# First token chunk of a gated projection split by hidden width: half of it between retention pairs, the rest after chunk two; weight conversion without Pool

## The chip, the cores and the metric

One core of one Trainium2 chip runs the whole program. The metric is device time in microseconds of one execution, median over several runs.

## What is computed

The reference is a retention layer followed by two feed-forward layers, in float32 (weights arrive as float64 words and are converted on the chip). Cut to what matters:

```python
# q, k, v: (4 batches, 8 heads, 576 positions, 64)
scores = q @ k.T / sqrt(64)
ret = scores * Dmat                 # Dmat[h,i,j] = gamma_h ** (i-j) for i >= j, else 0
x = (ret @ v) -> (2304 tokens, 512)
# feed-forward 1, d_ff = 1536
g = x @ w_gate;  val = x @ w_val
x = (g * sigmoid(g) * val) @ w_out  # (2304, 512)
# feed-forward 2, d_ff = 2048
r = maximum(x @ w_in, 0)
out = (r * r) @ w_out2              # (2304, 512)
```

## The kernel before, in words

**Retention.** Sixteen pairs (4 batches x 4 pairs of heads) run as a loop of 17 iterations; iteration n starts pair n and finishes pair n - 1. `load(n + 2)` issues the loads of q, k and v (`qk_sb`, `kv_sb`, four buffers each, L207 and L211) on SyncE's queue. `prep_state` scales k and q on Pool (L220, L224). `scores` multiplies k by q (L241) into a score tile `s` (two buffers of two PSUM banks), and VectorE multiplies it by the mask (L246). `state` accumulates k-v states (L265), ScalarE copies them to `sbd` (L270). `apply` multiplies q by the states and the masked scores by v (L283, L296), and ScalarE copies the result to `xy`, the activations, which stay on the chip, transposed (L301).

**Weight conversion.** A unit is a 128 x 512 tile of weights. There are 36 for phase one (for each of 12 slices f of the hidden width: gate g, value v, output o, in this order) and 32 for phase two (i and o for each of 16 slices). A unit is loaded as raw 64-bit words (L105; two buffers `raw_p`, and two more pieces lent from columns of `xy` while a chunk's activations there are no longer needed), then converted by the generator `conversion` in five steps: two ScalarE operations (L136, L137), then on VectorE a clamp (L139), a shift (L143), a merge of the sign bits (L145) and an addition of the low words, as two halves on VectorE (L151) for the first eight units and the odd ones, and as one operation on Pool (L153) for the other even ones. Then `parts_unit` splits the float into a rounded high part on ScalarE (L120) and the rest as a low part on Pool (L121). `pump(k)` advances the generator by k steps up to a limit; `ensure` runs it until a named unit exists.

**Projections.** Every product is done as three matmuls (high x high, high x low, low x high; `three`, L364 to L366). Tokens are in five chunks (four of 512 and one of 256). In phase one, a step (n, f) projects chunk n by the units g and v of slice f (24 matmuls of 512 columns), applies sigmoid on ScalarE (L405) and two products on VectorE (L407, L409), splits the hidden tile into high (L397, ScalarE) and low (L398, VectorE), and one step later `out1` multiplies it by unit o into four accumulators (12 matmuls); at the last f they are copied back to `xy`. The activations of the next chunk are split by `split_x` (L358, L359) behind the last projection of a chunk. Phase two works the same way with one projection a step, Relu and a square (L417, L419), and `out2`.

**Order.** The program order is the loop order below; the framework assigns each engine's queue at compile time from that order and a model of the times, so neighbours can change places. Eight units are converted during retention, one step at each of four places per iteration from iteration 3; the other 28 of phase one while chunk 0 is projected, four steps after each part of a step. The 32 units of phase two take the tiles that phase one's weights leave (`allowed`): 20 of them during the last chunk of phase one.

Weights live in two pools, `wa_p` (17 units, there from the start) and `wb_p` (19, in the space that retention's tiles leave).

Of the kernel before, what the change touches and what calls it, by code (L numbers as in the profile page):

```python
# [9 lines left out]
F32 = mybir.dt.float32  # L10
# [25 lines left out]
WA = 17  # L36
EARLY = 8
FROM = 3
PUMPS = {0: 1, 1: 4, 2: 1}
# [9 lines left out]
def retention_moe_kernel(  # L49
# [33 lines left out]
    order = [(1, what, f) for f in range(F1) for what in "gvo"]  # L83
# [24 lines left out]
    ring = {"n": 0}  # L108

    def weight_tiles():  # L110
        wp = wa_p if ring["n"] % (3 * F1) < WA else wb_p
        ring["n"] += 1
        hi = wp.tile([P, 512], F32R, tag="hi", name="w_hi")
        lo = wp.tile([P, 512], F32R, tag="lo", name="w_lo")
        return hi, lo

    def parts_unit(i):
        wf = w_t.pop(i).bitcast(F32)
        hi, lo = weight_tiles()
        nc.scalar.copy(hi, wf)  # L120
        nc.gpsimd.tensor_tensor(out=lo, in0=wf, in1=f32(hi), op=ALU.subtract)  # L121
        units[order[i]] = (hi, lo)

    def conversion():
        ts = nc.vector.tensor_scalar
        for i in range(len(order)):
# [22 lines left out]
            if i < EARLY or i % 2:  # L149
                for a in range(2):  # L150
                    nc.vector.tensor_tensor(out=w[:, a], in0=w[:, a], in1=low[:, a], op=ALU.add)  # L151
            else:
                nc.gpsimd.tensor_tensor(out=w, in0=w, in1=low, op=ALU.add)  # L153
# [23 lines left out]

    with ExitStack() as st:
# [133 lines left out]
        pumped["limit"] = 5 * EARLY  # L312
        for n in range(last + 2):
            new, old, nxt = n <= last, n > 0, n + 1 <= last
            fill = PUMPS[0] if n >= FROM else 0
            if n == FROM - 1:
                prefetch(1)
# [10 lines left out]
            if old:  # L328
                apply(n - 1, False)
# [8 lines left out]
            if old:  # L338
                apply(n - 1, True)


    wb_p = pool(ctx, "wb_p", 3 * F1 - WA)
    ps_g = pool(ctx, "ps_g", 2, space=PSUM)
    ps_a = pool(ctx, "ps_a", 1, space=PSUM)

    xs, xs_w = {}, []

    def split_x(ph, n, cc):
        t0, m = CHUNKS[ph][n]
        src = xy[:, cc, t0:t0 + m]  # L350
        if ph == 2 and n == 0:
            xs_w.append(weight_tiles())
        if ph == 2 and n % 2 == 0:
            hi, lo = cut(xs_w[cc], 0, m)
        else:
            hi = xs_p.tile([P, N], F32R, tag="xh", name="xh")[:, :m]
            lo = xs_p.tile([P, N], F32R, tag="xl", name="xl")[:, :m]
        nc.scalar.copy(hi, src)  # L358
        nc.vector.tensor_tensor(out=lo, in0=src, in1=f32(hi), op=ALU.subtract)  # L359
        xs[ph, n, cc] = (hi, lo)  # L360

    def three(dst, a, b, first, last):
        (ah, al), (bh, bl) = a, b
        nc.tensor.matmul(dst, ah, bh, start=first, stop=False)  # L364
        nc.tensor.matmul(dst, ah, bl, start=False, stop=False)  # L365
        nc.tensor.matmul(dst, al, bh, start=False, stop=last)  # L366

    def cut(pair, a, n):
        return tuple(x[:, a:a + n] for x in pair)

    def project(ph, n, f, *cols):
        for what, _ in cols:
            ensure((ph, what, f))
        parts = [
            (ps_g.tile([P, 512], F32, tag=tag, name=tag), units[ph, what, f]) for what, tag in cols
        ]
        last = f == (F1, F2)[ph - 1] - 1
        todo = [(ps, w, cc) for ps, w in parts for cc in range(CC)]
        split_after = ph == 1 and last and n + 1 < NCH
        if split_after:  # L380
            todo.sort(key=lambda x: x[2])
        for ps, w, cc in todo:
            three(ps[:, :CHUNKS[ph][n][1]], cut(w, cc * P, P), xs[ph, n, cc], cc == 0, cc == CC - 1)
        if split_after:
            for cc in range(CC):
                split_x(1, n + 1, cc)
        elif 3 <= f < 3 + CC and (ph, n) != (2, NCH - 1) and (ph == 2 or n == NCH - 1):
            split_x(2, (n + 1) % NCH, f - 3)
        return [ps[:, :CHUNKS[ph][n][1]] for ps, _ in parts]

    hs = {}

    def halves(key, t):
        m = t.shape[-1]
        hi = h_p.tile([P, N], F32R, tag="hh", name="h_hi")[:, :m]
        lo = h_p.tile([P, N], F32R, tag="hl", name="h_lo")[:, :m]
        nc.scalar.copy(hi, t)  # L397
        nc.vector.tensor_tensor(out=lo, in0=t, in1=f32(hi), op=ALU.subtract)  # L398
        hs[key] = (hi, lo)

    def hidden1(n, f):
        g, vv = project(1, n, f, ("g", "g"), ("v", "v"))
        yield
        t = t_p.tile([P, 512], F32, tag="t", name="t")[:, :CHUNKS[1][n][1]]
        nc.scalar.activation(out=t, in_=g, func=AF.Sigmoid)  # L405
        yield
        nc.vector.tensor_tensor(out=t, in0=g, in1=t, op=ALU.mult)  # L407
        yield
        nc.vector.tensor_tensor(out=t, in0=vv, in1=t, op=ALU.mult)  # L409
        yield  # L410
        halves((1, n, f), t)

    def hidden2(n, f):
        (ps,) = project(2, n, f, ("i", ("g", "v")[f % 2]))
        yield
        t = t_p.tile([P, 512], F32, tag="t", name="t")[:, :CHUNKS[2][n][1]]
        nc.scalar.activation(out=t, in_=ps, func=AF.Relu)  # L417
        yield
        nc.vector.scalar_tensor_tensor(  # L419
            out=t, in0=ps, scalar=0.0, in1=t, op0=ALU.max, op1=ALU.mult  # L420
        )
        yield
        halves((2, n, f), t)

    acc = {}

    def accs(n_acc):
        return [ps_a.tile([P, 512], F32, tag=f"a{i}", name=f"a{i}") for i in range(n_acc)]

    def out1(n, f):  # L430
        if f == 0:
            acc[1, n] = accs(CC)
        h = hs.pop((1, n, f))
        ensure((1, "o", f))
        w = units[1, "o", f]
        t0, m = CHUNKS[1][n]
        for cc in range(CC):
            three(acc[1, n][cc][:, :m], cut(w, cc * P, P), h, f == 0, f == F1 - 1)
        if f == F1 - 1:
            assert all(back is None for _, back in raw_t.values())  # L440
            for cc, a in enumerate(acc.pop((1, n))):
                dst = xy[:, cc, t0:t0 + m]
                if cc % 2:
                    nc.vector.tensor_copy(dst, a[:, :m])
                else:
                    nc.scalar.copy(dst, a[:, :m])

    def out2(n, f):
        if f == 0:
            acc[2, n] = accs(CHUNKS[2][n][1] // P)  # L450
        h = hs.pop((2, n, f))
        ensure((2, "o", f))
        w = units[2, "o", f]
        for tt in range(CHUNKS[2][n][1] // P):
            three(acc[2, n][tt], cut(h, tt * P, P), w, f == 0, f == F2 - 1)
        if f == F2 - 1:
            for tt, a in enumerate(acc.pop((2, n))):
                if tt % 2 == 0:
                    o = raw_p.tile([P, 1024], U32, tag="raw", name="o_sb").bitcast(F32)
                t = o[:, (tt % 2) * 512:][:, :512]  # L460
                if tt % 2:
                    nc.vector.tensor_copy(t, a)
                else:
                    nc.scalar.copy(t, a)
                r0 = CHUNKS[2][n][0] + tt * P
                nc.sync.dma_start(out=out[r0:r0 + P, :], in_=t)
# [9 lines left out]
    for cc in range(CC):  # L476
        split_x(1, 0, cc)
    prev = None
    for ph, n, f in steps:
# [9 lines left out]
        for _ in (hidden1, hidden2)[ph - 1](n, f):  # L489
# [66 lines left out]
```

## Time and profile before

| | us |
|---|---|
| median of 3 runs | 991.66 |
| lowest, highest | 989.36, 992.76 |
| the profiled execution, its own time | 991.55 |
| its span, first to last instruction | 989.8 |
| TensorE busy (share of the span) | 959.8 (97%) |
| VectorE busy | 458.6 (46%) |
| ScalarE busy | 351.8 (36%) |
| Pool busy | 172.2 (17%) |
| mean granted TensorE clock | 0.976 |
| first projection matmul starts at | 121.83 |

The span is that of one execution on the chip; the time of an execution is a little longer than its span. A busy share is an average over stages that have different limits: retention until 122 us, phase one with conversion until about 235, phase one without conversion until about 475, its last chunk and the start of phase two with conversion until about 630, then phase two alone. "Granted clock" is the share of TensorE's full clock that the throttle allowed.

### The profile page before, as it was taken

The numbers are of one execution on the slowest core, as the hardware profiler recorded it, in microseconds if no ns is written. First come the engines' busy times: TensorE is split into PE (matmuls) and PEld (weight loads), VectorE is DVE, ScalarE is ACT, GpSimd is POOL, SyncE is SP. The second block draws the span as 40 slices with busy tenths as digits, with TensorE's granted clock in tenths as the row PEclk, the third lists the DMA queues.
The fourth block names the chain that finished last, engine by engine and source line by source line (L and its number), as shares of the span: only waits on it lengthen the run. The fifth ranks groups of instructions, "written<-read, shape, count | busy, mean of one in ns | idle before, by whom it ended". The sixth has DMA issues, their size and how long they took to land.

```text
span 989.8 us, 12344 instructions
## 1 busy us (share of the span) xinstructions
PE 959.8 (97%) x5008; PEld 797.4 (81%) x5008; DVE 458.6 (46%) x711; ACT 351.8 (36%) x705; POOL 172.2 (17%) x138
## 2 busy tenths in 40 slices
PE   7899999989999999999999899999999999999998
PEld 5787788868888998888887678788888888888897
DVE  2877376973222323222699779424223322322232
ACT  3666565542111212111555456213223222322232
POOL 3467344520000000000245425100000000000000
PEclk9889799999999999999999899999999999999999
DMA  9788234420000000000133322001000100100010
GB/s 355 257 271 280 69 112 133 130 73 1 1 1 1 1 1 1 1 0 1 64 128 119 116 86 86 1 1 42 1 1 1 43 1 1 42 1 1 1 43 22
DMA packets 21689, 61.50 MB, mean 62 GB/s; under 512 B 2176, under 2 KB 3712, under 8 KB 21632
## 3 DMA queue, kind: packets, MB, share of 16 engines
q1 hardware_dynamic: 21632, 60.71, 18.3%
q8 instruction: 39, 0.64, 0.3%
q14 instruction: 18, 0.15, 0.0%
HBM read 55.98 MB, written 4.72 MB: 61 GB/s over the span
## 4 chain that ended last, share of the span: by engine, by line
PE 65%; DVE 12%; DMA 4%; ACT 2%; issue 2%; POOL 1%; SPq 0%; ACTq 0%; POOLq 0%
PE a L366 9%; PE a L365 9%; PE a L364 9%; PE v L366 6%; PE v L365 6%; PE v L364 6%; PE g L366 6%; PE g L365 6%; PE g L364 6%; DVE w L145 3%; DMA raw<-in_w 2%; DVE w L139 2%; DVE w L143 2%; DVE w L151 2%; DMA xy<-in_w 1%
## 5 line engine op out<-in xcount | busy, mean ns | idle before, releaser
L121 POOL TENSOR_TENSOR w_lo<-w,w_hi 128x512 fp32r<-128x512 f32 x68 | 92.5, 1364 | 363.1 <-ACT w_hi L120 363.1
L397 ACT CAST h_hi<-t 128x512 fp32r<-128x512 f32 (+1 forms) x140 | 80.9, 578 | 142.3 <-DVE t L409 89.2
L398 DVE TENSOR_TENSOR h_lo<-t,h_hi 128x512 fp32r<-128x512 f32 (+1 forms) x140 | 94.4, 674 | 77.7 <-ACT h_hi L397 77.3
L365 PE MATMUL g<-xl,w_hi 128*128 128x512 f32 (+1 forms) x304 | 113.9, 375 | 0.0
L364 PE MATMUL g<-xh,w_hi 128*128 128x512 f32 (+1 forms) x304 | 113.8, 374 | 0.0
L366 PE MATMUL g<-xh,w_lo 128*128 128x512 f32 (+1 forms) x304 | 113.5, 373 | 0.0
L364 PE MATMUL v<-xh,w_hi 128*128 128x512 f32 (+1 forms) x304 | 113.4, 373 | 0.0
L365 PE MATMUL v<-xl,w_hi 128*128 128x512 f32 (+1 forms) x304 | 113.3, 373 | 0.0
L366 PE MATMUL v<-xh,w_lo 128*128 128x512 f32 (+1 forms) x304 | 113.2, 372 | 0.0
L364 PE MATMUL a<-w_hi,h_hi 128*128 128x512 f32 x288 | 112.4, 391 | 0.2
L365 PE MATMUL a<-w_lo,h_hi 128*128 128x512 f32 x288 | 112.3, 390 | 0.0
L366 PE MATMUL a<-w_hi,h_lo 128*128 128x512 f32 x288 | 110.1, 390 | 1.7 <-DVE h_lo L398 1.7
L365 PE MATMUL a<-h_lo,w_hi 128*128 128x512 f32 (+1 forms) x240 | 91.0, 379 | 6.6 <-DVE h_lo L398 6.6
L364 PE MATMUL a<-h_hi,w_hi 128*128 128x512 f32 (+1 forms) x240 | 89.4, 377 | 4.3 <-ACT h_hi L397 4.3
L407 DVE TENSOR_TENSOR t<-g,t 128x512 f32<-128x512 f32 (+1 forms) x60 | 38.1, 635 | 114.8 <-ACT t L405 114.6
L366 PE MATMUL a<-h_hi,w_lo 128*128 128x512 f32 (+1 forms) x240 | 90.5, 377 | 0.0
L419 DVE SCALAR_TENSOR_TENSOR t<-g,t 128x512 f32<-128x512 f32 (+1 forms) x40 | 25.5, 637 | 106.1 <-ACT t L417 106.0
L405 ACT ACTIVATE t<-g 128x512 f32<-128x512 f32 (+1 forms) x60 | 33.0, 551 | 110.4 <-PE g L366 110.1
L419 DVE SCALAR_TENSOR_TENSOR t<-v,t 128x512 f32<-128x512 f32 (+1 forms) x40 | 25.5, 637 | 91.6 <-ACT t L417 91.3
L364 PEld LDWEIGHTS g<-xh,w_hi 128*128 128x128 f32 x304 | 57.8, 190 | 10.3
L365 PEld LDWEIGHTS g<-xl,w_hi 128*128 128x128 f32 x304 | 57.5, 189 | 10.3
L366 PEld LDWEIGHTS g<-xh,w_lo 128*128 128x128 f32 x304 | 57.6, 189 | 10.0
(70 smaller groups left out, 1627.2 us busy)
## 6 DMA issues: line engine op xcount, KB each, us to landing
raw<-in_w SPq DMA_DIRECT2D x45, 512.0 KB, 3.6
xy<-in_w SPq DMA_DIRECT2D x23, 512.0 KB, 3.6
kv_sb<-in_kv SPq DMA_DIRECT2D x16, 576.0 KB, 4.9
qk_sb<-in_qk SPq DMA_DIRECT2D x15, 576.0 KB, 5.8
out<-o_sb SPq DMA_DIRECT2D x18, 256.0 KB, 2.2
qs_sb<-in_qscale SPq DMA_DIRECT2D x4, 224.0 KB, 7.4
mask_sb<-in_mask SPq DMA_DIRECT2D x4, 128.0 KB, 7.0
qk_sb<-in_qk SPq DMA_DIRECT2D x1, 320.0 KB, 3.8
```

The costliest lines, as they stand in the source:

```text
L121: nc.gpsimd.tensor_tensor(out=lo, in0=wf, in1=f32(hi), op=ALU.subtract)
L139: ts(out=wf, in0=wf, scalar1=TINY, scalar2=HUGE, op0=ALU.max, op1=ALU.min)
L143: ts(out=w, in0=w, scalar1=3, scalar2=0x3FFFFFFF, op0=ALU.logical_shift_left, op1=ALU.bitwise_and)
L145: nc.vector.scalar_tensor_tensor(out=w, in0=high, scalar=0xC0000000, in1=w, op0=ALU.bitwise_and, op1=ALU.bitwise_or)
L364: nc.tensor.matmul(dst, ah, bh, start=first, stop=False)
L365: nc.tensor.matmul(dst, ah, bl, start=False, stop=False)
L366: nc.tensor.matmul(dst, al, bh, start=False, stop=last)
L397: nc.scalar.copy(hi, t)
L398: nc.vector.tensor_tensor(out=lo, in0=t, in1=f32(hi), op=ALU.subtract)
L405: nc.scalar.activation(out=t, in_=g, func=AF.Sigmoid)
L407: nc.vector.tensor_tensor(out=t, in0=g, in1=t, op=ALU.mult)
L419: nc.vector.scalar_tensor_tensor(out=t, in0=ps, scalar=0.0, in1=t, op0=ALU.max, op1=ALU.mult)
```

## The change

- The order of units becomes g and v of slices 0 to 5, o of slices 0 to 5, and then g, v, o of slices 6 to 11. During retention 14 units are converted (before: 8), two steps at each of four places per iteration from iteration 2.
- `hidden1_early`: at the end of each of the iterations 5 to 16 stand 12 projection matmuls of chunk 0: gate or value of one of the slices 0 to 5. The hidden tiles that result are kept, high and low, in six tiles of `wa_p`. Ahead of the first stands the split of chunk 0's activations, behind the last that of chunk 1.
- After retention comes chunk 1. Behind its first projection stand the 72 matmuls by o of slices 0 to 5 for chunk 0; their four accumulators are copied to two tiles of `raw_p` and written to DRAM (`part`). Behind chunk 1, chunk 0's activations are split again, its slices 6 to 11 are projected, `part` is loaded into chunk 0's columns of `xy`, and the second half of the accumulators is added to it there. Then chunks 2 to 4.
- PSUM during retention: the score tile has one buffer instead of two; the two banks that this leaves hold g and v. Loads `qk_p` and `kv_p`: three buffers instead of four.
- All conversion operations that were on Pool are on VectorE.

The diff, without the retention functions, which move down in the file unchanged:

```diff
-WA = 17
-EARLY = 8
-FROM = 3
-PUMPS = {0: 1, 1: 4, 2: 1}
+HALF = F1 // 2
+FROM = 5
+WA = 20
+UNITS_EARLY = WA - HALF
+PUMPS = {0: 2, 1: 4, 2: 1}
...
+    part_p = pool(ctx, "part_p", 1, space=bass.MemoryType.DRAM)
+    ps_g = pool(ctx, "ps_g", 1, space=PSUM)
+    late = False
...
-    order = [(1, what, f) for f in range(F1) for what in "gvo"]
+    order = [(1, what, f) for f in range(HALF) for what in "gv"] + [(1, "o", f) for f in range(HALF)]
+    order += [(1, what, f) for f in range(HALF, F1) for what in "gvo"]
...
+    in_a = {u: i < UNITS_EARLY or i >= 3 * F1 - HALF for i, u in enumerate(order[:3 * F1])}
+    homes = [in_a[u] for u in order[:3 * F1]] + [in_a[1, what, f] for f in range(F1) for what in "gvo"]
+    homes = iter(homes)
+    def weight_tiles(early=None):
+        wp = wa_p if early or next(homes) else wb_p
...
-        nc.gpsimd.tensor_tensor(out=lo, in0=wf, in1=f32(hi), op=ALU.subtract)
+        nc.vector.tensor_tensor(out=lo, in0=wf, in1=f32(hi), op=ALU.subtract)
...
-            if i < EARLY or i % 2:
-                for a in range(2):
-                    nc.vector.tensor_tensor(out=w[:, a], in0=w[:, a], in1=low[:, a], op=ALU.add)
-            else:
-                nc.gpsimd.tensor_tensor(out=w, in0=w, in1=low, op=ALU.add)
+            for a in range(2):
+                nc.vector.tensor_tensor(out=w[:, a], in0=w[:, a], in1=low[:, a], op=ALU.add)
...
+    part = part_p.tile([P, CC, N], F32, tag="part", name="part")
+    turn = {"g": 0, "v": 0}
+    def bank(tag):
+        turn[tag] += 1
+        return (ps_g2 if late and turn[tag] % 2 else ps_g).tile([P, 512], F32, tag=tag, name=tag)
...
-    def project(ph, n, f, *cols):
+    def project(ph, n, f, *cols, then=None):
...
+        parts = [(bank(tag), units[ph, what, f]) for what, tag in cols]
...
-        split_after = ph == 1 and last and n + 1 < NCH
-        if split_after:
+        if then is not None:
             todo.sort(key=lambda x: x[2])
...
-        if split_after:
+        if then is not None:
             for cc in range(CC):
-                split_x(1, n + 1, cc)
+                split_x(1, then, cc)
...
-    def halves(key, t):
+    def halves(key, t, early=False):
+        if early:
+            hi, lo = weight_tiles(early)
...
+    def hidden1_early(k):
+        f, what = k // 2, "gv"[k % 2]
+        if k == 0:
+            for cc in range(CC):
+                split_x(1, 0, cc)
+        (ps,) = project(1, 0, f, (what, what))
+        if what == "g":
+            early_t[f] = t = t_p.tile([P, 512], F32, tag="t", name="t")
+            nc.scalar.activation(out=t, in_=ps, func=AF.Sigmoid)
+        t = early_t[f]
+        nc.vector.tensor_tensor(out=t, in0=ps, in1=t, op=ALU.mult)
+        if what == "v":
+            halves((1, 0, f), early_t.pop(f), early=True)
+        if k == 2 * HALF - 1:
+            for cc in range(CC):
+                split_x(1, 1, cc)
...
     def out1(n, f):
-        if f == 0:
+        f0, f1 = ((f // HALF) * HALF, (f // HALF + 1) * HALF - 1) if n == 0 else (0, F1 - 1)
+        if f == f0:
             acc[1, n] = accs(CC)
...
-            three(acc[1, n][cc][:, :m], cut(w, cc * P, P), h, f == 0, f == F1 - 1)
+            three(acc[1, n][cc][:, :m], cut(w, cc * P, P), h, f == f0, f == f1)
+        if f < f1:
+            return
...
+            if n == 0 and f0 == 0:
+                if cc % 2 == 0:
+                    o = raw_p.tile([P, 1024], U32, tag="raw", name="part_sb").bitcast(F32)
+                dst = o[:, (cc % 2) * 512:][:, :512]
+            if n == 0 and f0:
+                nc.vector.tensor_tensor(out=dst, in0=a[:, :m], in1=dst, op=ALU.add)
+            elif cc % 2:
...
+            if n == 0 and f0 == 0:
+                nc.sync.dma_start(out=part[:, cc, :], in_=dst)
...
-        qk_p = pool(st, "qk_p", 4)
-        kv_p = pool(st, "kv_p", 4)
+        qk_p = pool(st, "qk_p", 3)
+        kv_p = pool(st, "kv_p", 3)
...
-        ps_s = pool(st, "ps_s", 2, space=PSUM)
+        ps_s = pool(st, "ps_s", 1, space=PSUM)
...
-        pumped["limit"] = 5 * EARLY
+        pumped["limit"] = 5 * UNITS_EARLY
...
-            fill = PUMPS[0] if n >= FROM else 0
-            if n == FROM - 1:
+            fill = PUMPS[0] if n >= FROM - 3 else 0
+            if n == FROM - 4:
                 prefetch(1)
...
+            if FROM <= n < FROM + 2 * HALF:
+                hidden1_early(n - FROM)
...
+    ps_g2 = pool(ctx, "ps_g2", 1, space=PSUM)
+    late = True
+    segments = [(1, 1, 0, F1), (1, 0, HALF, F1)] + [(1, n, 0, F1) for n in range(2, NCH)]
+    steps = [(ph, n, f, f == b - 1) for ph, n, a, b in segments for f in range(a, b)]
+    follows = {s[1]: t[1] for s, t in zip(segments, segments[1:])}
...
+    todo = [(1, 0, f) for f in range(HALF)]
...
+        if (ph, n, f) == (1, 0, HALF + 1):
+            nc.sync.dma_start(out=xy[:, :, CHUNKS[1][0][0]:][:, :, :CHUNKS[1][0][1]], in_=part)
+        step = hidden1(n, f, follows.get(n) if end else None) if ph == 1 else hidden2(n, f)
+        for _ in step:
             pump(PUMPS[ph])
-        if prev:
-            (out1 if prev[0] == 1 else out2)(*prev[1:])
-        prev = (ph, n, f)
+        for x in todo:
+            (out1 if x[0] == 1 else out2)(*x[1:])
+        todo = [(ph, n, f)]
```

More of the change, by code (lines that the diff above doesn't have):

```diff
@@ new lines, in three, with cut @@
+    def three(dst, a, b, first, last):
+        (ah, al), (bh, bl) = a, b
+        nc.tensor.matmul(dst, ah, bh, start=first, stop=False)
+        nc.tensor.matmul(dst, ah, bl, start=False, stop=False)
+        nc.tensor.matmul(dst, al, bh, start=False, stop=last)
+    def cut(pair, a, n):
+        return tuple(x[:, a:a + n] for x in pair)
+    def project(ph, n, f, *cols, then=None):
+        for what, _ in cols:
+            ensure((ph, what, f))
+        parts = [(bank(tag), units[ph, what, f]) for what, tag in cols]
+        last = f == (F1, F2)[ph - 1] - 1
+        todo = [(ps, w, cc) for ps, w in parts for cc in range(CC)]
+        if then is not None:
+            todo.sort(key=lambda x: x[2])
+        for ps, w, cc in todo:
+            three(ps[:, :CHUNKS[ph][n][1]], cut(w, cc * P, P), xs[ph, n, cc], cc == 0, cc == CC - 1)
+        if then is not None:
+            for cc in range(CC):
+                split_x(1, then, cc)
+        elif 3 <= f < 3 + CC and (ph, n) != (2, NCH - 1) and (ph == 2 or n == NCH - 1):
+            split_x(2, (n + 1) % NCH, f - 3)
+        return [ps[:, :CHUNKS[ph][n][1]] for ps, _ in parts]
@@ new lines, in retention_moe_kernel, with hidden1 @@
+    hs = {}
+    def halves(key, t, early=False):
+        m = t.shape[-1]
+        if early:
+            hi, lo = weight_tiles(early)
+        else:
+            hi = h_p.tile([P, N], F32R, tag="hh", name="h_hi")[:, :m]
+            lo = h_p.tile([P, N], F32R, tag="hl", name="h_lo")[:, :m]
+        nc.scalar.copy(hi, t)
+        nc.vector.tensor_tensor(out=lo, in0=t, in1=f32(hi), op=ALU.subtract)
+        hs[key] = (hi, lo)
+    def hidden1(n, f, then=None):
+        g, vv = project(1, n, f, ("g", "g"), ("v", "v"), then=then)
+        yield
+        t = t_p.tile([P, 512], F32, tag="t", name="t")[:, :CHUNKS[1][n][1]]
+        nc.scalar.activation(out=t, in_=g, func=AF.Sigmoid)
+        yield
+        nc.vector.tensor_tensor(out=t, in0=g, in1=t, op=ALU.mult)
+        yield
+        nc.vector.tensor_tensor(out=t, in0=vv, in1=t, op=ALU.mult)
+        yield
+        halves((1, n, f), t)
@@ new lines, in hidden2, with accs @@
+    def hidden2(n, f):
+        (ps,) = project(2, n, f, ("i", ("g", "v")[f % 2]))
+        yield
+        t = t_p.tile([P, 512], F32, tag="t", name="t")[:, :CHUNKS[2][n][1]]
+        nc.scalar.activation(out=t, in_=ps, func=AF.Relu)
+        yield
+        nc.vector.scalar_tensor_tensor(
+            out=t, in0=ps, scalar=0.0, in1=t, op0=ALU.max, op1=ALU.mult
+        )
+        yield
+        halves((2, n, f), t)
+    acc = {}
+    def accs(n_acc):
+        return [ps_a.tile([P, 512], F32, tag=f"a{i}", name=f"a{i}") for i in range(n_acc)]
@@ new lines, in out2 @@
+    def out2(n, f):
+        if f == 0:
+            acc[2, n] = accs(CHUNKS[2][n][1] // P)
+        h = hs.pop((2, n, f))
+        ensure((2, "o", f))
+        w = units[2, "o", f]
+        for tt in range(CHUNKS[2][n][1] // P):
+            three(acc[2, n][tt], cut(h, tt * P, P), w, f == 0, f == F2 - 1)
+        if f == F2 - 1:
+            for tt, a in enumerate(acc.pop((2, n))):
+                if tt % 2 == 0:
+                    o = raw_p.tile([P, 1024], U32, tag="raw", name="o_sb").bitcast(F32)
+                t = o[:, (tt % 2) * 512:][:, :512]
+                if tt % 2:
+                    nc.vector.tensor_copy(t, a)
+                else:
+                    nc.scalar.copy(t, a)
+                r0 = CHUNKS[2][n][0] + tt * P
+                nc.sync.dma_start(out=out[r0:r0 + P, :], in_=t)
@@ L413, in hidden2 @@
[L413 to L428, printed above, removed]
@@ L448, in out2 @@
[L448 to L466, printed above, removed]
@@ L474, in allowed @@
         return 3 * F1 + max(0, min(2 * (f - 1), 3 * (f - 1) - CC)) if ph == 1 else len(order)
[L476 to L479, printed above, removed]
+    todo = [(1, 0, f) for f in range(HALF)]
+    for ph, n, f, end in steps:
         pumped["limit"] = 5 * allowed(ph, n, f) + 7
-        if f == 1 and (ph, n) in ((1, 0), (1, NCH - 1), (2, 0)):
+        if f == 1 and (ph, n) in ((1, 1), (1, NCH - 1), (2, 0)):
             t0, m = CHUNKS[ph][n]
             loads["open"] = True
-            loads["cap"] = (3 * F1 if n == 0 and ph == 1 else len(order)) - 1
+            loads["cap"] = (3 * F1 if n == 1 else len(order)) - 1
             spare.extend(xy[:, c:c + 2, t0:t0 + m] for c in (0, 2))
```

110 lines of the change are left out of this document (32 added, 78 removed).

## The prediction

> **What bounds the kernel now.** I read the page first (shares and the chain that ended last), then the busy time by stretches of 25 us, then the stretches in which the granted clock is low, then TensorE's timeline at the seams. In the page, TensorE is busy almost all the time and ends the chain for 65%; VectorE is second with 12%.
>
> ```profile
> span 989.8 us, 12344 instructions
> PE 959.8 (97%) x5008; PEld 797.4 (81%) x5008; DVE 458.6 (46%) x711; ACT 351.8 (36%) x705; POOL 172.2 (17%) x138
> PE 65%; DVE 12%; DMA 4%; ACT 2%; issue 2%; POOL 1%; SPq 0%; ACTq 0%; POOLq 0%
> ```
>
> Busy time hides two things: a slow clock, and waits shorter than the pipeline. So I count the matmuls. These rows of the timeline (start us, length us) give the first projection, the spacing of the 512-column matmuls, that of the 256-column ones, and the last matmuls.
>
> ```profile
> 121.83 0.48 PE L364 MATMUL g<-xh,w_hi 128*128 128x512 f32 x1
> ...
> 201.21 0.39 PE L366 MATMUL v<-xh,w_lo 128*128 128x512 f32 x1
> 201.44 0.39 PE L364 MATMUL v<-xh,w_hi 128*128 128x512 f32 x1
> ...
> 980.12 0.28 PE L364 MATMUL v<-w_hi 128*128 128x256 f32 x1
> 980.24 0.28 PE L365 MATMUL v<-w_lo,w_hi 128*128 128x256 f32 x1
> ...
> 985.20 0.63 PE L366 MATMUL a<-w_hi,h_lo 128*128 128x512 f32 x2
> ```
>
> The program has 3360 projection matmuls of 512 columns (phase one 4 chunks x 36 units x 12; phase two 4 x 32 x 12, and 96 in its short chunk) and 624 of 256 columns. At 0.2273 us (201.21 to 201.44, to four digits the mean over a stretch without stalls) and 0.119 us that is 763.7 + 74.3 = 838.0 us. From the first, 121.8, to the last end, 985.8, are 864.0 us. So **26.0 us are lost** after retention, and 4.0 us lie behind the last matmul. Where:
>
> ```profile
> 200.00:225.00 25.00, 21.57 (x88) 17.14 (x87) 18.67 (x28) 10.86 (x19) 6.70 (x5) 0.93 0.18 63
> 250.00:275.00 25.00, 25.00 (x112) 20.72 (x111) 6.32 (x10) 4.04 (x7) 0.00 (x0) 1.00 0.00 1
> 525.00:550.00 25.00, 22.81 (x92) 18.16 (x92) 23.23 (x33) 12.53 (x21) 11.20 (x8) 0.93 0.38 126
> 550.00:575.00 25.00, 21.79 (x83) 17.19 (x82) 19.70 (x30) 11.82 (x20) 11.77 (x9) 0.86 0.38 125
> 575.00:600.00 25.00, 23.35 (x101) 18.39 (x100) 19.15 (x31) 14.03 (x25) 6.64 (x5) 1.00 0.18 65
> ```
>
> Columns are PE, weight loads, DVE, ACT, POOL, granted clock, DMA share, GB/s. At 250 to 275 nothing is missing. At 200 to 225, where the weights of phase one are still being converted, PE idles 3.4 us and loses half of another 3.4 us of half clock. At 525 to 600, the conversion for phase two, it idles 2.2 + 3.2 + 1.7 us, and the clock costs 5 us. I take about 10 us of the 26 for the first chunk and 16 for the second conversion.
>
> Before 121.8 stands retention. There the clock itself is the loss:
>
> ```profile
> 41.00:58.00 17.00, 16.92 (x119) 13.84 (x120) 12.34 (x20) 9.71 (x27) 7.08 (x6) 0.50 0.79 263
> 58.00:89.00 31.00, 29.38 (x339) 23.22 (x338) 23.63 (x34) 22.65 (x72) 22.41 (x18) 1.00 0.86 291
> 103.00:116.00 13.00, 13.00 (x94) 10.15 (x95) 3.04 (x7) 5.67 (x19) 4.35 (x4) 0.50 0.31 91
> ...
> 47.06 1.23 DVE L246 TENSOR_TENSOR p_sb<-s,mask_sb 128x1024 f32<-128x1024 f32 x1 [2.06 <-PE oa L296]
> ```
>
> A pair issues 64 matmul instructions. At full clock (58 to 89) 339 take 31.0 us, 5.85 us a pair with its waits; at half clock 94 take 13.0 us, 8.9 us a pair. The mask of pair 5 starts at 47.1, so iterations 5 to the end take 74.7 us, 28 of them at half clock.
>
> **The change, part by part.** *Twelve half steps move into iterations 5 to 16.* Each is 12 matmuls, 12 x 0.2273 = 2.73 us of PE, 32.7 in all, taken from the later 838.0. An iteration then costs 5.85 + 2.73 = 8.58 us of PE at full clock; 11 of them are 94.4, and the 17th, with only the rest of pair 15, about 4.5. With 3 us for the four input splits ahead of the first half step, retention ends at 47.1 + 94.4 + 4.5 + 3 = **149**, where no overlap at all would give 121.8 + 32.7 = 154.5. This uses the full clock: dense 512-column matmuls now stand in every iteration. The lower bound is 142 (5.5 us a pair, no split wait); the upper is taken from the rivals.
>
> *Conversion in retention, 14 units instead of 8, and all of it on VectorE.* The cost of one unit from these rows (min/median/max ns):
>
> ```profile
> L139 DVE TENSOR_SCALAR w<-w x68: 406/426/1531, 24.2 to 621.2; 128x512 f32<-128x512 f32 x68
> L143 DVE TENSOR_SCALAR w<-w x68: 405/427/1507, 24.7 to 622.2; 128x512 uint32<-128x512 uint32 x68
> L145 DVE SCALAR_TENSOR_TENSOR w<-raw,w x45: 673/692/1789, 25.4 to 622.6; 128x512 uint32<-128x512 uint32 x45
> L151 DVE CUSTOM_DVE_ANT_0 w<-raw,w x54: 403/418/1516, 26.3 to 624.8; 128x512 uint16<-128x512 uint16 x54
> L398 DVE TENSOR_TENSOR h_lo<-t,h_hi x140: 424/691/1848, 131.1 to 984.2; 128x512 fp32r<-128x512 f32 x112, 128x256 fp32r<-128x256 f32 x28
> ...
> 186.78 1.37 POOL L153 TENSOR_TENSOR w<-w,xy 128x512 uint32<-128x512 uint32 x1 [1.14 <-issue]
> ...
> 187.02 1.42 DVE L143 TENSOR_SCALAR w<-w 128x512 uint32<-128x512 uint32 x1
> ...
> 196.12 0.43 DVE L143 TENSOR_SCALAR w<-w 128x512 uint32<-128x512 uint32 x1
> ```
>
> Without POOL beside it a unit takes 0.426 + 0.427 + 0.692 + 2 x 0.418 + 0.691 (the low part, priced as h_lo, the same shapes) = 3.07 us. The same L143 takes 1.42 beside a POOL operation and 0.43 without. From iteration 2 on, 8 conversion steps of 5 a unit run per iteration: 1.6 units or 4.9 us, plus the two masks 1.5, plus about 1.0 for the half step, plus up to 1.4 of contention from POOL's remaining preparation: 8.8 us in iterations 5 to 10, level with PE's 8.58. If this cover were gone, the excess would be some 0.2 to 1 us in each of six iterations; it is inside the range.
>
> *The moved Pool work in the second conversion.* These are the groups between 478 and 630 (busy us, mean ns) and who waited there:
>
> ```profile
> L139 DVE TENSOR_SCALAR w<-w 128x512 f32<-128x512 f32 x30 | 21.9, 730 | 11.5 <-ACT w L137 11.4
> L145 DVE SCALAR_TENSOR_TENSOR w<-raw,w 128x512 uint32<-128x512 uint32 x19 | 20.0, 1054 | 0.5
> L143 DVE TENSOR_SCALAR w<-w 128x512 uint32<-128x512 uint32 x30 | 19.7, 656 | 0.8
> L398 DVE TENSOR_TENSOR h_lo<-t,h_hi 128x512 fp32r<-128x512 f32 x19 | 15.2, 800 | 1.5 <-ACT h_hi L397 1.4
> L145 DVE SCALAR_TENSOR_TENSOR w<-xy,w 128x512 uint32<-128x512 uint32 x11 | 13.4, 1218 | 0.3
> ...
> ACT w L137 <- POOL w_lo L121: 11.9, 13, 1.9
> ...
> ACT w_hi L120 <- POOL w L153: 6.6, 9, 2.1
> ...
> PE a L365 <- DVE h_lo L398: 4.0, 3, 2.3
> ```
>
> VectorE gains 32 x 0.691 + 15 x 0.836 = 34.6 us and loses what is above the medians: 9.1 + 6.9 + 6.9 + 2.1 + 5.8 = 30.8 us. Its load is unchanged, but ACT's 18.5 us of waits on POOL go, and so do single operations of 1.8 us ahead of h_lo. What is late next is VectorE's own queue: in the last chunk of phase one, 20 units x 3.07, 12 hidden steps x 2.1 and four splits are 90 us beside 98 us of PE. I take 10 of the 16 us as remaining; bounds 4 and 25.
>
> *Chunk two first.* Its 12 steps need only 22 units instead of 28, and 16.4 us of PE work (72 matmuls of the stored hidden tiles) come before weight 18 is needed. Of 10 us I keep 4.
>
> *The parked half.* Four 256 KB writes, one 1 MB return, four copies and four adds. They use the two raw buffers while the next two raw loads hold them, and the accumulators wait for it; the next projection, 24 x 0.2273 = 5.5 us, covers. I add 2 us for this and for the one additional seam between chunks, bounds 0 and 6. The extra four input splits (about 0.7 us each on VectorE) lie beside matmuls at the seam. On SyncE's queue the writes stand ahead of raw loads that are not needed for five steps; nothing.
>
> *Three instead of four load buffers.* The kv load of pair n + 2 must wait for pair n - 1, at the end of iteration n.
>
> ```profile
> raw<-in_w SPq DMA_DIRECT2D x45, 512.0 KB, 3.6
> ...
> kv_sb<-in_kv SPq DMA_DIRECT2D x16, 576.0 KB, 4.9
> ```
>
> It lands in 4.9 us, POOL prepares it in about 2.3, and it has one iteration, 8.58: covered by 1.4 us, and less in iterations 1 to 4, where the raw loads compete.
>
> **Sum**, by the profiled execution: 149 + (838.0 - 32.7) + 16 + 4.0 = 974.3 span; its own time, 991.55, lies 1.75 above its span 989.8 and 0.1 below the median 991.66. So **976 us**, 1.6% faster.
>
> **Rivals.**
>
> *The clock stays as it is in retention.*
>
> ```profile
> 45.00:50.00 5.00, 5.00 (x35) 3.94 (x36) 2.23 (x4) 3.33 (x8) 2.03 (x2) 0.50 0.61 199
> ```
>
> Here PE is marked busy for all 5 us and the clock stays at half, so busy rows alone do not release it. If 37% of the time (28 of 74.7) stays at half clock, 11 x 8.23 + 4.5 = 95 us of work take 95 / 0.815 = 117, retention ends at 167, and the total is 167 + 805.3 + 16 + 4 + 1.75 = 994: no change. [...] Against it: in 58 to 89 the clock held with retention alone. [...]
>
> *VectorE keeps its slow times without POOL.* Then a unit costs the means, about 4.05 us, the conversions lose 31 us instead of 16, total 991. The clear 0.43 above speaks against it.
>
> *Slower: the single score buffer.* The second scores of a pair now wait until VectorE has read the first, twice a pair. The mask takes 1.23 and 0.28 us, and with one conversion operation of 0.69 ahead of each, 2.9 us are exposed if nothing lies between; behind PE's waiting score stand the state matmuls and the half step.
>
> ```profile
> PEld s L241 <- DVE p_sb L246: 3.0, 4, 2.0
> ```
>
> With two buffers PE's loads already waited 3.0 us for it. Half exposed, 1.45 x 16 = 23 us, gives 976 + 23 = 999; it turns slower (above 994.6) from 1.2 us a pair. Against it: states and applications stand between the scores. [...]
>
> *Better:* retention at 142 and 6 us lost give 142 + 805.3 + 6 + 4 + 1.75 = 959.
>
> **How the numbers follow.** Likeliest case (966 to 986) 0.56; better 0.15; no change (clock or slow VectorE) 0.16; slower 0.13. A change of 0.3% (3 us) is what can be told from none here. A part of the no-change case, 986 to 988.6, counts as faster. Faster 0.74, same 0.12, slower 0.14. The range leaves out the ends of the better and the slower case: 961 to 996.
>
> **What would show it.** First late projection (24 matmuls in a row after the last half step) at 145 to 153; clock near 1.00 from iteration 5 on; L143 at 0.43 after retention; PE above 24 us in each 25 us of the second conversion. Wrong: half clock between half steps, scores that wait for p_sb over 1 us a pair, half steps that wait for weights, or VectorE full while PE waits for h_lo.

## The result, and the profile after

The changed kernel takes 954.83 us (median; 952.73 to 956.86), the kernel before 990.55 beside it: a ratio of 0.9637, 95% interval 0.9608 to 0.9666. It is faster by 36 us. The forecast, 976, lay 15.7 us below the 991.66 known when it was made; the measured time lies below the range, 961 to 996.

The page of the profiled execution (954.54 us, span 952.8): totals, the chain that ended last, and the granted clock in forty slices.

```profile
span 952.8 us, 12345 instructions
PE 931.5 (98%) x5008; PEld 775.8 (81%) x5008; DVE 462.9 (49%) x847; ACT 352.4 (37%) x709; POOL 40.3 (4%) x40
PEclk9899999999999999999999999999999999999999
PE 92%; DMA 3%; DVE 2%; ACT 2%; issue 1%; SPq 0%; POOL 0%; POOLq 0%; ACTq 0%
```

TensorE now ends the chain for 92% (65% before), VectorE for 2% (12%), with VectorE's busy time almost unchanged (462.9 against 458.6 us). The same stretches of 25 us as before, in the two conversions (PE, weight loads, DVE, ACT, POOL, clock, DMA share, GB/s):

```profile
200.00:225.00 25.00, 25.00 (x112) 20.69 (x111) 22.08 (x47) 15.75 (x27) 0.00 (x0) 1.00 0.48 145
...
500.00:525.00 25.00, 25.00 (x112) 20.71 (x111) 23.10 (x50) 15.15 (x26) 0.00 (x0) 1.00 0.43 139
525.00:550.00 25.00, 25.00 (x112) 20.71 (x111) 20.90 (x44) 13.15 (x23) 0.00 (x0) 1.00 0.39 128
550.00:575.00 25.00, 25.00 (x112) 20.68 (x111) 21.95 (x44) 17.69 (x32) 0.00 (x0) 1.00 0.29 101
```

All 25 us are filled, at full clock, while VectorE is busy for up to 23.1 of 25. The seam behind retention and the last matmuls, from the timeline:

```profile
148.66 0.33 PE L465 MATMUL ob<-p_sb,kv_sb 64*64 64x64 f32 x4
148.92 0.50 PE L210 MATMUL g<-xh,w_hi 128*128 128x512 f32 x1
...
947.98 0.62 PE L212 MATMUL a<-w_hi,h_lo 128*128 128x512 f32 x2
```

Retention ends at 148.9, and the last matmul at 948.6. Retention itself, in three stretches:

```profile
32.00:39.00 7.00, 5.86 (x44) 4.85 (x44) 5.67 (x13) 5.41 (x15) 0.05 (x1) 0.51 0.68 239
39.00:115.00 76.00, 72.87 (x575) 55.68 (x575) 61.54 (x107) 45.76 (x121) 18.55 (x15) 1.00 0.61 198
115.00:148.00 33.00, 32.41 (x394) 26.01 (x396) 9.01 (x12) 16.33 (x63) 10.22 (x10) 1.00 0.47 151
```

From 39 us on the clock is full. From 115 to 148 stands retention alone: 394 instructions of 64 a pair in 33 us are 5.36 us a pair. From 39 to 115 there are 575 instructions, 162 of them projections (0.2273 us each, 36.8 us) and 413 of retention (6.5 pairs at 5.36, 34.6 us), together 71 of 76 us: TensorE is nearly full there.

To compare the experiments I split each trace into three terms that sum to the end of its last matmul: 838.0 us of projections; the stalls behind the last retention matmul (all spacings of projection matmuls beyond 0.2273 us); and the rest, which is what retention costs beyond the projections done meanwhile ("net"). The last column is the time at half clock up to the last retention matmul.

| kernel | median us | end of last matmul | stalls behind retention | retention, net | half clock in it |
|---|---|---|---|---|---|
| before | 990.55 | 985.8 | 22.6 | 125.3 | 34.1 |
| changed | 954.83 | 948.6 | 0.6 | 110.0 | 6.8 |
| before, no Pool in conversion | 961.75 | 955.2 | 0.4 | 116.8 | 17.1 |
| before, only low parts off Pool | 969.15 | 965.0 | 2.8 | 124.2 | 27.3 |
| before, only additions off Pool | 985.11 | 982.3 | 17.5 | 126.8 | 34.1 |
| changed, Pool back | 987.67 | 979.0 | 27.5 | 113.5 | 13.7 |
| changed, Pool computes the low parts again for nobody | 993.16 | 990.1 | 33.3 | 118.8 | 17.1 |
| before, one score buffer | 1003.46 | 998.6 | 28.3 | 132.3 | 51.2 |
| before, three load buffers | 1004.36 | 1000.0 | 27.4 | 134.6 | 51.2 |
| before, no Pool, one score buffer, three load buffers | 972.04 | 966.0 | 0.4 | 127.6 | 54.6 |
| changed, half steps behind the last pair | 962.31 | 953.2 | 1.1 | 114.1 | 17.1 |
| changed, one conversion step a place | 957.97 | 953.2 | 0.4 | 114.8 | 13.7 |
| changed, four load buffers | 954.85 | 947.9 | 1.0 | 108.9 | 3.4 |
| changed, four load buffers, conversion from iteration 3 | 951.23 | 945.7 | 0.4 | 107.3 | 13.7 |

Of the 37.2 us between the first two rows, 22.0 are stalls that are gone and 15.3 retention. The terms are those of one profiled execution each, which lay up to 3.2 us from the median of its kernel; ratios below are of the timed runs.

The prediction counted 26.0 us as lost behind retention. It took the first projection matmul of the kernel before, at 121.8 us, for the end of retention, but 49 projection matmuls start ahead of retention's last ones:

```profile
136.65 0.33 PE L296 MATMUL ob<-p_sb,kv_sb 64*64 64x64 f32 x4
136.91 0.50 PE L365 MATMUL g<-xl,w_hi 128*128 128x512 f32 x1
```

So 3.4 of the 26.0 us belong to retention, and 22.6 are stalls: 6.3 ahead of 475 us, while the first chunk is projected, and 16.2 in the second conversion.

### The profile page after: what moved, and what is told of

Same layout as the page of the kernel before. It is cut to its first block, busy times and chain, and to the rows that moved or that the text cites. A ratio compares the mean times of both kernels' runs of the same rounds, so it can differ in the third digit from the quotient of the medians.

```text
span 952.8 us, 12345 instructions
## 1 busy us (share of the span) xinstructions
PE 931.5 (98%) x5008; PEld 775.8 (81%) x5008; DVE 462.9 (49%) x847; ACT 352.4 (37%) x709; POOL 40.3 (4%) x40
## 3 DMA queue, kind: packets, MB, share of 16 engines
q1 hardware_dynamic: 22224, 62.81, 19.7%
## 4 chain that ended last, share of the span: by engine, by line
PE 92%; DMA 3%; DVE 2%; ACT 2%; issue 1%; SPq 0%; POOL 0%; POOLq 0%; ACTq 0%
PE a L210 12%; PE a L211 12%; PE a L212 12%; PE v L212 8%; PE v L210 8%; PE v L211 8%; PE g L210 8%; PE g L212 8%; PE g L211 8%; DMA raw<-in_w 2%; PE s L410 2%; PE oa L452 2%; PE ob L434 1%; PE oa L465 1%; DMA ks_sb<-in_kscale 1%; DVE w L159 1%
## 5 line engine op out<-in xcount | busy, mean ns | idle before, releaser
L243 ACT CAST h_hi<-t 128x512 fp32r<-128x512 f32 (+1 forms) x134 | 77.1, 575 | 114.8 <-DVE t L255 63.3
L244 DVE TENSOR_TENSOR h_lo<-t,h_hi 128x512 fp32r<-128x512 f32 (+1 forms) x134 | 85.1, 636 | 67.7 <-ACT h_hi L243 67.4
L210 PE MATMUL g<-xh,w_hi 128*128 128x512 f32 (+1 forms) x304 | 114.1, 375 | 0.0
L211 PE MATMUL v<-xl,w_hi 128*128 128x512 f32 (+1 forms) x304 | 113.5, 373 | 0.0
L211 PE MATMUL a<-h_lo,w_hi 128*128 128x512 f32 (+1 forms) x216 | 79.0, 366 | 0.0
L212 PE MATMUL a<-h_hi,w_lo 128*128 128x512 f32 (+1 forms) x216 | 78.9, 365 | 0.0
L210 PE MATMUL a<-h_hi,w_hi 128*128 128x512 f32 (+1 forms) x216 | 77.2, 366 | 0.0
L253 DVE TENSOR_TENSOR t<-g,t 128x512 f32<-128x512 f32 (+1 forms) x54 | 34.0, 630 | 85.9 <-ACT t L251 85.8
L210 PEld LDWEIGHTS v<-xh,w_hi 128*128 128x128 f32 x304 | 57.3, 189 | 9.9 <-issue 0.2
L212 PEld LDWEIGHTS v<-xh,w_lo 128*128 128x128 f32 x304 | 57.3, 188 | 10.0
L211 PEld LDWEIGHTS v<-xl,w_hi 128*128 128x128 f32 x304 | 57.3, 188 | 9.9 <-issue 0.2
```

## The experiments

**Conversion off Pool, nothing else.**

```diff
-        nc.gpsimd.tensor_tensor(out=lo, in0=wf, in1=f32(hi), op=ALU.subtract)
+        nc.vector.tensor_tensor(out=lo, in0=wf, in1=f32(hi), op=ALU.subtract)
...
-            if i < EARLY or i % 2:
-                for a in range(2):
-                    nc.vector.tensor_tensor(out=w[:, a], in0=w[:, a], in1=low[:, a], op=ALU.add)
-            else:
-                nc.gpsimd.tensor_tensor(out=w, in0=w, in1=low, op=ALU.add)
+            for a in range(2):
+                nc.vector.tensor_tensor(out=w[:, a], in0=w[:, a], in1=low[:, a], op=ALU.add)
```

> The kernel before with one part of the change: all conversion operations of Pool go to VectorE; order, split and buffers stay. Theory A (most of the gain is Pool's removal: the slow VectorE operations and ACT's waits on Pool made the 26 us of stalls behind retention): the stalls fall from 26 to under 6 us, no half clock behind retention, 966 to 972 us. Theory B (most of the gain is the work moved under retention and the earlier weights): the conversions stay as late as before, 983 to 990 us.

961.75 us, ratio 0.9722 (0.9682 to 0.9761): 29 of the 36 us come with this part alone, some 4 us more than even theory A asked for, since retention also gains 8.5 us (net, 125.3 to 116.8). A stretch in the second conversion:

```profile
525.00:550.00 25.00, 25.00 (x112) 20.71 (x111) 22.36 (x48) 14.62 (x26) 0.00 (x0) 1.00 0.36 129
```

The weights are converted in the old order, eight units early, and TensorE hardly stalls (0.4 us in all): the weights' order was not what it waited for. Theory B falls.

**The changed kernel with Pool back.** The same lines reversed, in the changed kernel (with 8 in place of `EARLY`).

> The changed kernel with the conversion back on Pool as before (low parts, and the addition of every other unit from the ninth). Theory A: 15 to 25 us slower than the changed kernel, 970 to 980, with half clock in the second conversion. Theory B: 956 to 962, since fewer units are left for the first projected chunk; only the second conversion loses a little.

987.67 us, ratio 0.9975 (0.9948 to 1.0003) to the kernel before: slower than expected by either theory, and no longer told apart from the kernel before. Its stalls are back in both conversions:

```profile
225.00:250.00 25.00, 22.25 (x84) 17.80 (x84) 22.63 (x33) 14.04 (x24) 13.06 (x11) 0.86 0.34 105
...
525.00:550.00 25.00, 22.40 (x90) 17.48 (x89) 21.57 (x32) 13.06 (x23) 13.16 (x11) 0.93 0.35 122
```

So the split by itself does not save the stalls; with Pool in the conversion it is worth about 3 us, no more than the interval leaves open. In the two traces it does shorten retention, net, by 11.8 us (125.3 to 113.5), but the stalls grow by 4.9 (22.6 to 27.5).

**Only the low parts, and only the additions, off Pool.** One of the two edits above each, in the kernel before.

> The kernel before with only the low parts on VectorE; the addition of every other unit stays on Pool. If each Pool operation costs by the VectorE time that it slows and the hop that it adds, the low parts (92 of Pool's 134 us of conversion) carry two thirds of the 29 us: 968 to 975. If only the hop of the addition back into ScalarE and the low part matters, the gain is under 10 us: above 981.

> The kernel before with only the additions on VectorE; the low parts stay on Pool. By slowed VectorE time one third of the 29 us: 978 to 985. If the hop of the addition is what matters: 966 to 973.

969.15 (0.9793, 0.9738 to 0.9848) and 985.11 (0.9959, 0.9930 to 0.9987): 21 and 5 us, together 25 of the 29. The low parts carry most, as they do of the conversion's time on Pool (92 of 134 us). Both times are those of the first case of their expectations, 985.11 by a hair outside it; the hop of the addition is not what matters.

**Is it the time that VectorE loses beside Pool, or the hop?** The hop is the step of a unit's chain through Pool, for which ScalarE and the next unit wait. Here is the changed kernel, and Pool computes a subtraction of the old size beside each unit's low part, into a tile that no other instruction reads.

```diff
+    shadow = keep.tile([P, 512], F32, tag="shadow", name="shadow")
...
         nc.vector.tensor_tensor(out=lo, in0=wf, in1=f32(hi), op=ALU.subtract)
+        nc.gpsimd.tensor_tensor(out=shadow, in0=shadow, in1=f32(hi)[:, :512], op=ALU.subtract)
```

> The changed kernel, and Pool in addition computes each unit's low part again into a scratch tile that nobody reads: 68 operations of Pool's old kind and time, started like them by the high part, with no engine waiting for them. If what Pool cost is VectorE's time beside it (slow clamps, shifts, merges and low parts): 968 to 978, two thirds or more of the 33 us that Pool's return cost. If it is the hop through Pool, for which ScalarE and the next unit waited: 954 to 958.

993.16 us, 1.0015 (0.9999 to 1.0031) of the kernel before: 38 us slower than the changed kernel, though nobody waits for these 68 operations, and 15 us beyond the first case of the expectation. TensorE, VectorE and ScalarE execute the same instructions in the same order in both traces, so no other order of the queues explains it. The groups of VectorE in the second conversion (478 to 630 us), first of the changed kernel, then of this one, and the one of Pool (busy us, mean ns):

```profile
L130 DVE TENSOR_TENSOR w_lo<-w,w_hi 128x512 fp32r<-128x512 f32 x28 | 19.2, 687 | 1.9 <-ACT w_hi L129 1.7
...
L154 DVE SCALAR_TENSOR_TENSOR w<-raw,w 128x512 uint32<-128x512 uint32 x17 | 11.7, 686 | 0.1
L152 DVE TENSOR_SCALAR w<-w 128x512 uint32<-128x512 uint32 x26 | 11.0, 424 | 0.5
...
L154 DVE SCALAR_TENSOR_TENSOR w<-xy,w 128x512 uint32<-128x512 uint32 x10 | 6.9, 686 | 0.0
```

```profile
L133 DVE TENSOR_TENSOR w_lo<-w,w_hi 128x512 fp32r<-128x512 f32 x30 | 35.8, 1195 | 0.3 <-ACT w_hi L132 0.2
L156 DVE TENSOR_SCALAR w<-w 128x512 uint32<-128x512 uint32 x29 | 16.4, 566 | 0.5
L158 DVE SCALAR_TENSOR_TENSOR w<-raw,w 128x512 uint32<-128x512 uint32 x18 | 16.2, 900 | 0.1
...
L158 DVE SCALAR_TENSOR_TENSOR w<-xy,w 128x512 uint32<-128x512 uint32 x11 | 11.4, 1039 | 0.0
```

```profile
L134 POOL TENSOR_TENSOR shadow<-shadow,w_hi 128x512 f32<-128x512 f32 x30 | 51.9, 1729 | 316.4 <-ACT w_hi L132 316.3
```

The low part takes 1195 ns instead of 687, the merges 900 and 1039 instead of 686, the shifts 566 instead of 424. TensorE's waits from 478 to 660 us (total, times, longest) are of the old kind, on the hidden tile's two parts; in the kernel before they were 4.0, 3.1 and 1.7 us:

```profile
PE a L215 <- DVE h_lo L248: 7.6, 7, 2.1
PE a L214 <- ACT h_hi L247: 4.1, 6, 1.2
PE a L216 <- DVE h_lo L248: 2.0, 3, 0.7
```

VectorE's time beside Pool, with no hop, is enough for stalls of this size. (By the table the stalls grow by 32.7 us. The 8.8 that retention loses besides need not be VectorE's: there the scratch operations also stand in Pool's queue among its preparations of k and q.) But this kernel's VectorE also carries the low parts, beside a Pool operation that starts with each, so it is fuller than in the kernel before (24.3 and 24.1 of 25 us here, 23.2 and 19.7 there in the same stretches):

```profile
525.00:550.00 25.00, 22.22 (x98) 17.84 (x97) 24.30 (x43) 11.71 (x21) 7.28 (x6) 1.00 0.32 106
550.00:575.00 25.00, 20.85 (x87) 15.88 (x86) 24.14 (x40) 11.85 (x20) 10.19 (x6) 1.00 0.36 116
```

How the old 22.6 us divide between slow operations and hop is therefore not measured. The old trace speaks for the first: from 478 to 640 us its chain that ended last runs through VectorE for 81 us and through Pool's own operations for 3. Why VectorE's operations take longer beside Pool's, no run shows: the low parts and merges, which read two tensors in SBUF, do so here (1195 against 687 ns, 900 and 1039 against 686), and so do the shifts, which read one (566 against 424).

**One score buffer, three load buffers, one at a time, in the kernel before.**

```diff
-        ps_s = pool(st, "ps_s", 2, space=PSUM)
+        ps_s = pool(st, "ps_s", 1, space=PSUM)
```

> The kernel before with one score buffer instead of two, nothing else: the price of that part by itself. The prediction's slower rival: 1.2 us or more a pair, 1010 us or more. Other theory: state matmuls and applications between the two scores cover the mask, within 3 us of before, 988 to 994.

```diff
-        qk_p = pool(st, "qk_p", 4)
-        kv_p = pool(st, "kv_p", 4)
+        qk_p = pool(st, "qk_p", 3)
+        kv_p = pool(st, "kv_p", 3)
```

> The kernel before with three load buffers instead of four for q and k and for k and v, nothing else. As predicted, the late kv load is covered by an iteration: 989 to 994. If Pool's preparation of the next pair comes late in the first, load-bound iterations: 995 to 1000.

1003.46 (1.0133, 1.0099 to 1.0167) and 1004.36 (1.0137, 1.0095 to 1.0179): each costs 13 to 15 us by itself, the first between the values that were expected, the second above them. In the traces 7.0 and 9.3 us of that are retention, net, and 5.7 and 4.8 are stalls behind it. With one score buffer, retention runs at half clock for 51 us:

```profile
80.00:116.00 36.00, 33.03 (x229) 25.96 (x230) 19.99 (x27) 18.01 (x54) 19.43 (x16) 0.54 0.59 202
```

The waits that the slower rival asked for are not there: from 10 to 140 us TensorE's matmuls wait for the mask to read the scores for 2.4 us in all, 2.1 in the kernel before. What grew are their waits for ScalarE's copies of the states (`sbd`), from 2.0 to 12.9 us (total, times, longest):

```profile
PE ob L265 <- ACT sbd L270: 7.7, 10, 3.3
PE ob L283 <- ACT sbd L270: 5.2, 3, 3.2
PE s L241 <- DVE p_sb L246: 2.4, 3, 1.2
```

Why those copies come later is open.

With three load buffers the loads come later: that of k and v for pair 4 is issued at 30.3 us, behind two raw weight loads in an entry of 3.3 us; in the kernel before at 21.5. Pairs are counted from 0, and the mask of pair 3 starts at 37.8, in the kernel before at 31.1. But it does not wait for a load:

```profile
26.88 3.32 SPq L105 DMA_DIRECT2D raw<-in_w  x2
...
27.15 0.93 PE L241 MATMUL s<-qk_sb 64*128 64x128 f32 x10
...
28.10 1.70 DVE L151 CUSTOM_DVE_ANT_0 w<-raw,w 128x512 uint16<-128x512 uint16 x2
...
30.30 0.38 SPq L211 DMA_DIRECT2D kv_sb<-in_kv  x1
...
32.20 0.98 DVE L139 TENSOR_SCALAR w<-w 128x512 f32<-128x512 f32 x1 [2.40 <-ACT w L137]
...
37.43 0.41 DVE L143 TENSOR_SCALAR w<-w 128x512 uint32<-128x512 uint32 x1
37.76 1.21 DVE L246 TENSOR_TENSOR p_sb<-s,mask_sb 128x1024 f32<-128x1024 f32 x1
```

The scores of pair 3 are done at 28.1; between them and the mask stand ten operations of VectorE's queue, nine of conversion and one split of activations; the third of them waits 2.4 us for ScalarE. The framework assigns the queues anew for each program, and here it put the mask behind them. So what these two buffers cost, alone, is measured; through which wait is not.

**Both buffers without Pool: the change without its split.**

> The kernel before without Pool in the conversion, and with the single score buffer and the three load buffers, but without the split: what these two buffers cost where Pool no longer slows VectorE. Alone in the kernel before they cost 13 and 15 us. If that price comes from VectorE operations that Pool slows ahead of the masks: 962 to 968, close to 961.75. If it comes from the waits themselves, and the dense half steps cover it in the changed kernel: 975 to 990.

972.04 us (0.9831, 0.9777 to 0.9885), 10 us more than without Pool alone, between the two expectations. From here to the changed kernel, 972 to 955, only the split and what goes with it (14 early units, the order, the parked half) is left: 17 us, all in retention (127.6 to 110.0 net). The two stretches 40 to 80 and 80 to 116, of this kernel and then of the changed one:

```profile
40.00:80.00 40.00, 36.64 (x372) 29.91 (x368) 32.80 (x51) 24.99 (x75) 14.62 (x12) 0.80 0.73 257
80.00:116.00 36.00, 33.59 (x337) 26.53 (x333) 22.75 (x39) 21.54 (x70) 11.94 (x10) 0.81 0.64 216
```

```profile
40.00:80.00 40.00, 37.09 (x299) 27.92 (x299) 33.41 (x59) 26.02 (x67) 10.32 (x9) 1.00 0.56 186
80.00:116.00 36.00, 35.79 (x284) 27.80 (x282) 27.13 (x48) 19.59 (x53) 7.98 (x6) 1.00 0.67 215
```

The clock is 0.80 without the half steps and 1.00 with them. Half clock in retention falls from 54.6 to 6.8 us; half of the difference, 24 us, is more than the 17.6 by which the net term falls. (Half is an estimate: in the kernel before, between 555 and 558 us, 512-column matmuls follow 0.43 us apart at a clock of 0.50, against 0.2273 at 1.00.) That it is the half steps that hold the clock is not shown: no kernel here changed the clock alone, without Pool and with the old buffers there are 17.1 us of half clock and no half steps, and the kernel with the shortest retention (107.3, the last row of the table) has 13.7.

**Half steps behind the last pair.**

```diff
-            if FROM <= n < FROM + 2 * HALF:
-                hidden1_early(n - FROM)
+        for k in range(2 * HALF):
+            hidden1_early(k)
```

> The changed kernel with its twelve half steps behind the last pair in the program instead of one in each iteration; everything else stays. If the gain of the split is that dense matmuls fill retention's waits: the framework can pull forward only a part, and the total is 965 to 985. If the split is worth only the work's early weights: 953 to 958.

962.31 us (0.9725, 0.9695 to 0.9754), between the two expectations: the framework still pulls the half steps forward (168 projection matmuls start before 140 us, in the changed kernel before 116), and 17.1 us are at half clock. It is 7 us slower than the changed kernel; how much a split without any overlap would cost is not answered by it.

**One conversion step at each place.**

```diff
-PUMPS = {0: 2, 1: 4, 2: 1}
+PUMPS = {0: 1, 1: 4, 2: 1}
```

> The changed kernel with one conversion step at each place of retention instead of two, so that the 12 to 14 units are spread over all 15 iterations. Theory C (in the first half of retention the raw loads, two buffers, and ScalarE's queue that waits for them hold up the pairs): the first nine iterations get shorter, retention ends at 140 to 145, 946 to 951 us. Rival D (VectorE's load of conversions is what fills that half, or the work is only moved): retention ends where it did, 952 to 958 us.

957.97 us (0.9666, 0.9632 to 0.9700): theory C falls, it is 3 us slower. The time is rival D's, but retention does not end where it did: it ends at 153.6, later by 4.7 us. Between 100 and 125 TensorE is left with 22.6 of 25 us and 180 instructions:

```profile
100.00:125.00 25.00, 22.60 (x180) 16.82 (x180) 20.50 (x36) 15.88 (x41) 4.41 (x4) 1.00 0.58 212
```

**Four load buffers again, and conversions one iteration later.**

```diff
-        qk_p = pool(st, "qk_p", 3)
-        kv_p = pool(st, "kv_p", 3)
+        qk_p = pool(st, "qk_p", 4)
+        kv_p = pool(st, "kv_p", 4)
```

> The changed kernel with four load buffers as before. If the three buffers are what makes its first four iterations slower (fourth mask at 38.6 us, before 31.1), they shorten by 3 to 6 us and the total is 948 to 952. If the single score buffer or the conversion from iteration 2 does it, the total stays at 953 to 957.

```diff
-            fill = PUMPS[0] if n >= FROM - 3 else 0
-            if n == FROM - 4:
+            fill = PUMPS[0] if n >= FROM - 2 else 0
+            if n == FROM - 3:
```

> The changed kernel with four load buffers, and conversions from iteration 3 instead of 2. If the first four iterations of the changed kernel are slow because raw weight loads and conversions stand beside the first pairs' loads: the fourth mask comes at 31 to 33 us, and the total is 948 to 952. If TensorE is full behind them anyway and the work only moves: 953 to 957.

Four buffers alone: 954.85 (0.9634, 0.9593 to 0.9675), no difference from the changed kernel, though they were worth 15 us in the kernel before. The fourth mask does come at 32.4, and the masks stay 4 to 14 us ahead up to that of pair 11; from pair 13 on the lead is 1 us. By 116 us 154 projection matmuls are done, in the changed kernel 168: TensorE is nearly full there, and the work only moves. With conversions from iteration 3 as well: 951.23 us (0.9606, 0.9584 to 0.9627), the fastest here. Its four runs (950.8 to 952.0) lie below all of the changed kernel's (952.7 to 956.9), but the intervals of the two ratios overlap; some 3 us is a likely gain, not a certain one. The fourth mask at 34.8 is later than the 31 to 33 that the first case asked for, so its reason is not confirmed.

## Why the prediction was right or wrong

*The end of retention* was forecast at 149 and measured at 148.9, but not as argued; that the two agree is luck. The iterations do not take 8.58 us each: the masks of the first nine follow 9 to 14 us apart, the last ones 5.4. The framework pulls the half steps forward (the first of their matmuls starts at 24.1 us, the mask of pair 5, in whose iteration they begin in the program, at 61.8), and by 148.9 there are 168 projection matmuls done, not 144. In the terms of the table the forecast was 149 - 32.7 = 116.3 us net, and 110.0 were measured; the 24 more matmuls are 5.5 of these 6.3 us.

*The stalls* are the step that failed: "I take 10 of the 16 us as remaining", "of 10 us I keep 4" and "I add 2 us" made 16.0, and 0.6 were measured: 15.4 of the 21.5 us between the forecast span, 974.3, and the measured one, 952.8. The rows quoted there had the cause: a shift of 1.42 us beside Pool and 0.43 without, and TensorE waiting for h_lo. The prediction worked out from them that VectorE's load would stay the same, and took that load for a reason why stalls remain. In the changed kernel VectorE is as full as before (23.1 of 25 us), and TensorE has no wait from 478 to 640 us. Behind retention no operation of VectorE takes longer than 0.7 us there; in the kernel before 47 took more than 1 us, every one of them beside a Pool operation. The scratch operations show the reverse: Pool work that nobody waits for brings stalls back, 33 us of them. (The 10 us for the first chunk were also too many to begin with: 6.3, as said under the table.)

*"Its load is unchanged"* was right for VectorE's sum: the clean unit of 3.07 us was measured as such (0.423 + 0.424 + 0.686 + 2 x 0.420 + 0.687 = 3.06), and VectorE's total rose by 4 us. So the rival that VectorE keeps its slow times, 991, falls.

*The clock in retention.* The rival with half clock, 994, was refuted: 1.00 from 39 us on. The prediction's reason for the full clock, dense matmuls in every iteration, was the author's estimate. What a half step of 2.73 us does for the clock by itself the trace does not show: between the half steps stand retention's matmuls, and TensorE is busy for 72.9 of the 76 us from 39 to 115. How much of retention's 15.3 us the clock brought is not shown by itself; Pool's removal alone brought 8.5.

*The buffers.* "Covered by 1.4 us" was wrong as a statement on three load buffers: alone they cost 15 us. Loads do come later behind raw loads, which the same paragraph mentioned, but the trace does not show that this is the price. The slower rival had the single score buffer cost 1.2 us or more a pair, by scores that wait for the mask. Alone it costs 13 us, 7.0 of them in retention, which is 0.4 a pair, and the wait that the rival named hardly grew (2.1 to 2.4 us in all). In the changed kernel the fourth load buffer is worth nothing (954.85 against 954.83); what a second score buffer would be worth there, no run shows.

*The parked half and the additional seam*: all stalls together are 0.6 us, so nothing of the 2 us came.

*The direction* was right, and so was the mechanism of VectorE's clean operations; what they leave of the stalls was mis-sized, nothing instead of 16 us. The full clock came as forecast, but its share in the gain stays open.

## What to carry to other kernels

Where operations of a busy engine take longer beside those of a second one (here a shift of VectorE 1.42 us beside Pool and 0.43 without), its busy sum does not tell the stalls: here the sum stayed (458.6 and 462.9 us) and the stalls vanished (22.6 and 0.6 us). That the longest single operation ahead of the critical consumer is the number to count fits the traces (up to 1.85 us with the stalls, 0.7 without), but no run tested it apart from the sum. What a moved engine's work costs others can be tested apart from who waits for it, by running it for nobody. The price of a buffer in one kernel says little for another: three load buffers instead of four cost 15 us in the kernel before, and nothing in the changed kernel (954.83 against 954.85), where TensorE is busy for 72.9 of 76 us of retention.

## What the runs showed of the hardware that was not expected

Sixty-eight Pool subtractions of 128 x 512, read by nobody, cost 38 us of 955: VectorE's busy time rose from 462.9 to 527.0 us. Pool's operations took longer too: in the kernel before the low part took 1.26 to 1.31 us in the four of 68 cases with no VectorE operation beside it, and up to 1.84 us in the others. The scratch operations took 1729 ns in the second conversion, the low parts on Pool in the kernel before 1353 in the same stretch. Not every VectorE operation took longer: the products that read g or v from PSUM have a mean of 0.68 us in the second conversion with the scratch operations and of 0.69 in the changed kernel, and none of them in the kernel before reaches 0.70 us, with or without Pool beside it.

A TensorE that is marked busy can run at half clock for long: 13.00 of 13.00 us from 103 to 116 in the kernel before, at a granted clock of 0.50. Kernels without half steps ran retention at half clock for 17 to 55 us, kernels with them for 3 to 17.
